# DeltaNet with a max-out network: state times keys and queries in one product of 128 stationary columns, together with a wider fine solve, a new start and the output in the other half

## Chip, cores and metric

One core of one Trainium2 chip. The metric is the device time of one execution in microseconds. Each kernel was run four to six times (once profiled) beside runs of the kernel before on the same chip. The rounds of experiments ran on different chips, so runs of different rounds are compared by their ratio to the kernel before. "PE" is TensorE, "PEld" its weight loads, "DVE" VectorE, "ACT" ScalarE, "POOL" GpSimd, "SP" SyncE.

## The reference

Four sequences of 768 tokens and 8 heads of 48 go through a delta rule; its output, 3072 tokens of 384, goes through a max-out network with three input matrices and one output matrix.

```python
for t in range(S):                       # S = 768, D = 48, per batch (4) and head (8)
    y[:, :, t] = einsum('bhd,bhde->bhe', q_t, state)
    v_old = einsum('bhde,bhd->bhe', state, k_t)          # k normalized
    state = state + beta_t * einsum('bhd,bhe->bhde', k_t, v_t - v_old)
x = y.transpose(0, 2, 1, 3).reshape(B * S, H * D)
out = maximum(maximum(x @ w1, x @ w2), x @ w3) @ w_out
```

## The kernel before

The sequence is cut into 12 chunks of 64 tokens. Two chunks make a group of 512 tokens for the feed-forward network (FFN); six groups follow each other. The FFN products of one group (`p_h`, `p_o`) are mixed with the delta-rule links of the next two chunks. A chunk needs the inverse of a triangular matrix: DVE solves small diagonal blocks, then PE puts the blocks together (`p_e`, `p_f`, the "fine solve", and `p_z`, `p_j`). Then the state is multiplied with the chunk's keys (`p_k`) and queries (`p_q`); the first is subtracted from the values, the second kept for the output.

```python
def times_state(kqt, i, name):            # i = 0: keys, 1: queries
    p_b = ps_two(name)
    for j in range(NP):
        for g in range(2):
            for par in range(2):
                for bb in range(2):
                    c0 = (g * NP + j) * D
                    nc.tensor.matmul(
                        p_b[rows(bb), par, c0 : c0 + D],
                        kqt[g][rows(par), j, bb ^ g, i],   # 64 rows x 64 columns, stationary
                        st[rows(par), bb ^ g, g, j],       # 64 rows x 48 columns, moving
                    )
    return p_b[...]
...
def old_k(c):                             # one subtraction on DVE, 128x768
    ... out=rhs, in0=rhs, in1=times_state(kqt, 0, "p_k"), op=ALU.subtract
def old_q(c):                             # one copy on ACT, 128x768
    ... nc.scalar.copy(heads(qs), times_state(kqt, 1, "p_q"))
...
# start: the fine solves of chunks 0 and 1 are interleaved, ahead of the first FFN product
halves_z(0); halves_u(0); halves_z(1); join_z(0); halves_u(1); join_u(0); join_z(1)
old_k(0); old_q(0); new(0); join_u(1); to_y(0); to_x(0)
```

(The last three lines are shortened: weight conversions and loads between them are left out.) `rows(0)` and `rows(1)` are the two halves of 64 partitions, so the four combinations of `par` and `bb` use four tiles of 64x64 of the PE array.

## Time and profile before

| | before |
|---|---|
| time, median of 4 runs | 616.4 us (615.9 to 617.9) |
| first FFN product `p_h` starts | 76.0 us |
| `p_e` of chunk 2 starts | 127.8 us |
| last `p_o` of the first group ends | 210.7 us |
| from there to the last `p_o` of the sixth group | 399.5 us |
| granted clock after 155.7 us | 1.0 without a break up to 613.1 us |

The times in the table are read from the start and end of single instructions in the trace. The last two rows are a steady part in which PE is busy 98% of the time, at full clock.

### The profile page before, as it was taken

The numbers are of one execution on the slowest core, as the hardware profiler recorded it, in microseconds if no ns is written. First come the engines' busy times: TensorE is split into PE (matmuls) and PEld (weight loads), VectorE is DVE, ScalarE is ACT, GpSimd is POOL, SyncE is SP. The second block draws the span as 40 slices with busy tenths as digits, with TensorE's granted clock in tenths as the row PEclk, the third lists the DMA queues.
The fourth block names the chain that finished last, engine by engine and source line by source line (L and its number), as shares of the span: only waits on it lengthen the run. The fifth ranks groups of instructions, "written<-read, shape, count | busy, mean of one in ns | idle before, by whom it ended". The sixth has DMA issues, their size and how long they took to land.

```text
span 614.8 us, 19609 instructions
## 1 busy us (share of the span) xinstructions
PE 559.4 (91%) x8794; PEld 342.7 (56%) x8794; DVE 304.8 (50%) x713; ACT 160.8 (26%) x292; POOL 77.4 (13%) x108
## 2 busy tenths in 40 slices
PE   6644667978999999999999999999999999999996
PEld 5534556867655665555655546655556455554443
DVE  1652599328739962389542499432595422101110
ACT  3231545236613142121233121232111111110000
POOL 5360274114400000000000000000000000000000
PEclk9655569897999999999999999999999999999999
DMA  8985257652673254421452321522103100010002
GB/s 156 178 203 123 73 137 141 137 145 70 125 123 65 48 121 74 87 49 31 90 105 58 63 54 27 108 54 61 21 14 82 28 2 3 13 39 1 0 1 52
DMA packets 140820, 45.46 MB, mean 74 GB/s; under 512 B 126400, under 2 KB 136384, under 8 KB 140736
## 3 DMA queue, kind: packets, MB, share of 16 engines
q1 hardware_dynamic: 137744, 41.45, 33.2%
q0 software_dynamic: 880, 2.36, 1.4%
q8 instruction: 69, 1.13, 0.8%
q10 hardware_dynamic: 2112, 0.39, 0.4%
q14 instruction: 15, 0.12, 0.1%
HBM read 29.98 MB, written 14.16 MB: 72 GB/s over the span
## 4 chain that ended last, share of the span: by engine, by line
PE 70%; DVE 16%; issue 5%; POOL 3%; DMA 2%; SPq 2%; ACT 1%; POOLq 0%; ACTq 0%; DVEq 0%
PE p_h L707 37%; PE p_o L731 15%; DVE y_bl L453 4%; DVE tmp L449 4%; PE p_g L356 3%; PE p_t L334 3%; PE p_k L597 2%; DVE h L717 1%; PE p_q L597 1%; PE p_y L660 1%; PE p_z L564 1%; SPq L112 1%; PE p_s L643 1%; PE p_u L625 1%; PE p_e L521 1%
## 5 line engine op out<-in xcount | busy, mean ns | idle before, releaser
L707 PE MATMUL p_h<-xt,w_sb 128*128 128x512 f32 (+1 forms) x702 | 301.3, 575 | 2.0 <-DVE xt L693 1.3
L707 PEld LDWEIGHTS p_h<-xt,w_sb 128*128 128x128 f32 x702 | 130.9, 195 | 124.8 <-issue 116.6
L717 DVE TENSOR_TENSOR h<-h,p_h 128x512 f32<-128x512 f32 (+1 forms) x78 | 50.2, 644 | 142.9 <-PE p_h L707 142.8
L731 PE MATMUL p_o<-wo_sb,h 128*128 128x384 f32 x288 | 97.1, 490 | 2.5 <-DVE h L717 2.4
L731 PEld LDWEIGHTS p_o<-wo_sb,h 128*128 128x128 f32 x288 | 53.3, 190 | 41.3 <-DVE h L717 6.5
L453 DVE TENSOR_TENSOR y_bl<-y_bl,tmp 128x31 f32<-128x31 f32 (+20 forms) x154 | 52.7, 342 | 4.2
L449 DVE TENSOR_TENSOR tmp<-x_bl,y_bl 128x31 f32<-128x31 f32 (+20 forms) x154 | 51.8, 337 | 4.2
L715 ACT COPY h<-p_h 128x512 f32<-128x512 f32 (+1 forms) x39 | 21.5, 551 | 122.1 <-PE p_h L707 122.1
L356 PE MATMUL p_g<-kqt 64*64 64x64 f32 (+1 forms) x1280 | 32.1, 249 | 11.0 <-ACT kqt L340 10.5
L275 POOL TENSOR_TENSOR v_t<-v_t,nrm 128x768 f32<-128x768 f32 x12 | 18.2, 1513 | 180.7 <-DMA v_t<-in_v_dram 93.7
L356 PEld LDWEIGHTS p_g<-kqt 64*64 64x64 f32 x1280 | 27.6, 149 | 18.1 <-ACT kqt L340 14.0
L739 ACT COPY o_sb<-p_o 128x384 f32<-128x384 f32 x24 | 11.5, 480 | 88.3 <-PE p_o L731 85.3
L340 ACT COPY kqt<-p_t 128x512 f32<-128x512 f32 (+1 forms) x32 | 25.2, 797 | 31.2 <-PE p_t L334 31.0
L509 DVE STREAM_TRANSPOSE t<-ut 32x256 f32<-32x256 f32 x32 | 13.9, 434 | 23.1 <-DMA ut<-y_d 22.8
L236 POOL TENSOR_TENSOR w_sb<-mant,up 128x384 int32<-128x384 int32 x18 | 18.7, 1036 | 20.6 <-DVE mant L232 11.6
L334 PE MATMUL p_t<-ident,kpad 128*128 128x128 f32 x96 | 17.0, 308 | 4.3 <-DVE pt L366 2.1
L366 DVE TENSOR_TENSOR pt<-p_g,mask 128x512 f32<-128x512 f32 x24 | 16.1, 686 | 9.1 <-PE p_g L356 8.8
L374 ACT COPY at<-p_g 128x512 f32<-128x512 f32 x20 | 11.6, 586 | 32.2 <-DVE pt L366 29.7
L213 POOL TENSOR_SCALAR mant<-mant 128x384 f32<-128x384 f32 x24 | 12.7, 531 | 51.9 <-ACT mant L209 51.8
L625 PEld LDWEIGHTS p_u<-v_t,ut 64*64 64x64 f32 x768 | 13.2, 142 | 8.9 <-issue 7.7
L334 PEld LDWEIGHTS p_t<-ident,kpad 128*128 128x128 f32 x96 | 12.5, 156 | 8.8 <-issue 5.5
L643 PEld LDWEIGHTS p_s<-u,kpad 64*64 64x64 f32 x704 | 12.2, 144 | 9.1 <-issue 5.3
(97 smaller groups left out, 503.1 us busy)
## 6 DMA issues: line engine op xcount, KB each, us to landing
w_bits<-in_moe_w_dram SPq DMA_DIRECT2D x18, 384.0 KB, 3.6
at_d<-at SPq DMA_DIRECT2D x36, 128.0 KB, 2.5
qpad<-in_q_dram SPq DMA_DIRECT2D x48, 96.0 KB, 3.1
v_t<-in_v_dram SPq DMA_DIRECT2D x24, 192.0 KB, 4.3
out_dram<-o_sb SPq DMA_DIRECT2D x48, 96.0 KB, 2.2
kpad<-in_k_dram SPq DMA_DIRECT2D x44, 96.0 KB, 3.4
x_bl<-at_d SPq DMA_DIRECT2D x22, 128.0 KB, 3.6
y_d<-y_bl SPq DMA_DIRECT2D x11, 256.0 KB, 3.0
```

The costliest lines, as they stand in the source:

```text
L236: nc.gpsimd.tensor_tensor(out=dst.bitcast(I32), in0=mant_v.bitcast(I32), in1=up_v, op=ALU.add)
L334: nc.tensor.transpose(p_t[:, i, j * 128 : (j + 1) * 128], src[:, 2 * j : 2 * j + 2], ident,)
L340: nc.scalar.copy(kqt.rearrange("p j b i t -> p i (j b) t")[:, some], p_t.rearrange("p i (x t) -> p i x t", t=C)[:, some],)
L356: nc.tensor.matmul(p_g[rows(bb ^ (g * i)), par, c0 : c0 + C * (1 + whole)], kq[:, 0], kq if whole else kq[:, i],)
L449: nc.vector.tensor_tensor(out=t_v, in0=row.to_broadcast(t_v.shape), in1=column.to_broadcast(t_v.shape), op=ALU.mult,)
L453: nc.vector.tensor_tensor(out=rest, in0=rest, in1=t_v, op=ALU.subtract)
L597: nc.tensor.matmul(p_b[rows(bb), par, c0 : c0 + D], kqt[g][rows(par), j, bb ^ g, i], st[rows(par), bb ^ g, g, j],)
L625: nc.tensor.matmul(p_v[rows(bb ^ g), g, h], ut[c % NU][rows(bb), g, h], rhs[rows(bb), g, h],)
L707: nc.tensor.matmul(p_h, w_sb[i][:, t, f * 128 : (f + 1) * 128], xt[:, t, lo : lo + w], start=(t == 0), stop=(t == KT - 1),)
L715: nc.scalar.copy(h, p_h)
L717: nc.vector.tensor_tensor(out=h, in0=h, in1=p_h, op=ALU.max)
L731: nc.tensor.matmul(p_o, hs[f][:, i * 128 : (i + 1) * 128], wo_sb[:, f], start=(f == 0), stop=(f == FT - 1),)
```

## The change

Its intent is to halve the number of products of state with keys and queries, by taking keys and queries side by side as one stationary operand of 128 columns. Queries then come out in the other half of the partitions, so the output moves there too. With it come four other edits: the fine solve works on tiles of 64 rows in place of 32; chunk 1's solve moves behind the first FFN product; PE's order in the first group is fixed by hand; most weight fetches are issued by ACT, and the loads of beta by POOL. Smaller ones are not shown: the fine solve writes its tile without four copies on ACT, the turned keys and queries are copied in two pieces, loads of the start are in another order, and 18 products of no use, which keep PE busy at the start, stand in place of 24.

```diff
-    def times_state(kqt, i, name):
-        ... (64 columns, once for keys, once for queries; one eviction each)
+    def old(c):
+        ...
+        for g in range(2):
+            p_b = ps_two("p_b")
+            ...
+            for j in range(NP):
+                for par in range(2):
+                    for bb in range(2):
+                        kq = kqt[g][rows(par), j, bb ^ g]
+                        nc.tensor.matmul(
+                            p_v[:, par, bb, j],
+                            kq.rearrange("p i t -> p (i t)"),   # 128 columns
+                            st[rows(par), bb ^ g, g, j],
+                        )
+            for bb in range(2):        # evictions: 64 partitions x 384 each
+                ... nc.scalar.copy(to[r_q], p_v[r_q, :, bb])
+            for bb in range(2):
+                ... nc.vector.tensor_tensor(out=rhs, in0=rhs, in1=p_v[r, :, bb], op=ALU.subtract)
 (fine solve)
-                        r = block(bb, f)                          # 32x32, 16 columns
-                        nc.tensor.matmul(p_v[r, g, h], at[g][r, h, BL*f : BL*(f+1)], d[r, g, h, HB:])
+                r = rows(bb)                                      # 64x64, 32 columns
+                nc.tensor.matmul(p_v[r, g, h], at[g][r, h], second[r, g, h, :, 1])
 (output)
-                    p_v[rows(bb), g, h], pt[g][rows(bb ^ g), h], ...
+                    p_v[rows(1 - bb), g, h], pt[g][rows(bb ^ g), h], ...
 (start)
-    halves_z(1) ... halves_u(1) ... join_z(1) ... join_u(1)       # before the first FFN product
+    FIRST = {0: "s0 e1 T2", 1: "f1 P2 T3", 2: "z1 P3", 3: "k1 j1", ...}   # behind it
+    by_hand.enter_context(tc.manual_schedule(engines={mybir.EngineType.PE}))  # first group
-            nc.sync.dma_start(out=st...)      # fetch of weights
+            queue.dma_start(out=st...)        # queue = nc.scalar
```

## The prediction

> **What bounds the kernel now.** I read the stage table (busy time of each engine in chosen stretches) first, cut where the chain of waits shows the phases change: the triangular solve of chunks 0 and 1 (40 to 75.4 us), the first feed-forward group up to chunk 2's state product (to 119.6), the rest of that group (to 206.8), and groups 1 to 5.
>
> ```profile
> core 0: us, PE busy (x) PEld busy (x) DVE busy (x) ACT busy (x) POOL busy (x), PEclk, DMA share, GB/s
> 40.00:75.40 35.40, 19.20 (x934) 17.06 (x934) 12.15 (x24) 12.77 (x25) 9.14 (x14) 0.50 0.49 108
> 75.40:119.60 44.20, 34.55 (x672) 27.79 (x674) 35.86 (x83) 18.60 (x39) 20.72 (x24) 0.82 0.66 136
> 119.60:206.80 87.20, 81.06 (x1783) 55.21 (x1784) 54.52 (x130) 34.30 (x68) 19.31 (x22) 0.92 0.50 106
> 206.80:614.80 408.00, 400.25 (x5032) 221.67 (x5031) 182.19 (x419) 81.64 (x135) 11.84 (x9) 1.00 0.23 47
> ```
>
> After 206.8 us PE is busy 98% at full clock: any PE time added or removed there moves the end one for one. Before that PE has holes and a low clock, and DVE (36 of 44 us) is the limit between 75 and 107 us, where the chain runs along it. So the change has to be judged twice: in a latency-bound start and in a PE-bound rest.
>
> The chain of waits in the start shows how the first solve spends its time:
>
> ```profile
> 46.11 1.03 PE p_f L541 x59
> 47.14 1.65 issue
> 48.78 1.09 PE p_f L541 x67
> ...
> 50.68 2.25 issue
> 52.94 0.99 PE p_e L521 x46
> ...
> 54.78 3.80 issue
> ```
>
> The "issue" pieces, with 1.57 and 2.12 us more up to 66 us, make 11.4 us in which PE waits for nothing that the profile shows, among streams of very small products.
>
> For the product in question I read the timeline and then the groups by form:
>
> ```profile
> 474.32 1.15 PE L597 MATMUL p_k<-st,kqt 64*64 64x48 f32 x64
> 475.29 1.11 PE L597 MATMUL p_q<-st,kqt 64*64 64x48 f32 x64
> 476.33 1.98 PE L707 MATMUL p_h<-xt,w_sb 128*128 128x512 f32 x4
> ```
>
> ```profile
> L707 PEld LDWEIGHTS p_h<-xt,w_sb 128*128 128x128 f32 x702 | 130.9, 195 | 124.8 <-issue 116.6 <-DVE h L717 0.9 <-DVE x_bl L435 0.5
> L597 PEld LDWEIGHTS p_k<-st,kqt 64*64 64x64 f32 x704 | 11.3, 135 | 7.2 <-issue 6.1 <-DVE h L717 0.8 <-DVE t L527 0.3
> L564 PEld LDWEIGHTS p_z<-ut,at 32*32 32x32 f32 x512 | 5.3, 105 | 3.0 <-issue 3.0
> ```
>
> A product of the program is two MATMULs here (64 for the 32 in p_k). Keys and queries together take 476.33 - 474.32 = 2.01 us a chunk, 15.7 ns an instruction. p_h streams 512 columns in 0.43 us (2.58 us for six in the chain), 0.84 ns a column, so 48 columns would be 40 ns, or 10 ns an instruction with four tiles at work. The moving side is therefore not the limit. A weight load lasts 105, 135 and 195 ns for 32, 64 and 128 columns: about 0.9 ns for each stationary column, on top of a fixed part. 64 columns are some 55 to 60 ns, and a quarter of that is the 15 ns seen. **The product is bound by loading stationary columns, four tiles side by side.**
>
> [...]
>
> **The change part by part.**
>
> 1. State times keys and queries: 32 products a chunk with 128 stationary columns instead of 64 with 64. Half the instructions, but each loads 128 columns[...]. [...] **+1.6 us a chunk**, 11 chunks. Eight fall to groups 1 onward: **+12.8 us**, all on the path. Three fall to the start.
>
> 2. Its evictions: one subtraction (950 ns) and one copy (799 ns) of 128x768 become four each of 64 partitions x 384, about 0.55 and 0.48 us (a 128x384 copy takes 480 ns). That adds 1.25 us on DVE and 1.1 on ACT a chunk. Chunks with five microseconds of FFN work before their next product hide it, but DVE is nearly full in each group that still solves (7.5 of 8 us between 266 and 274), where PE already waits 1.0 us for it: about 1 us for each of three groups, **+3 us**. The split kqt copies (two of some 0.6 us for one of 1.0) are hidden.
>
> 3. Fine solve: 64 products a stage on 32-row blocks become 32 with 64 columns in two diagonal tiles. Instructions halve (512 to 256 MATMULs for two chunks' p_e), fill's four ACT copies (0.615 us each) go. PE time per stage rises: 64 x 29 ns = 1.9 us at full clock against about 1.1 now, twice that cold. DVE gains a second 0.71 us transpose.
>
> 4. Start: y_d and its read-back all go through SP. Now POOL issues half of them behind v_t, mant and w_sb work (dg at 39.9 us, first p_e at 43.0 to 43.7). I expect ut0 at 41 to 42. Chunk 1's solve leaves the path to the first FFN product. Chunk 0 alone, largely cold: p_e 3.5, copy 0.6, p_f 3.5, corners 1, p_z 1, transposes and copy 2.5, p_j and its eviction 2, p_u 1.7, u 0.6, p_y 1.7, y 0.6, p_x and xt 2, waits for DVE's in-order queue 1.5 and issue holes 1.5: 24 us, first p_h near 65 instead of 75.4, **10 us earlier**.
>
> 5. What takes this back: chunk 1's solve and its DVE work now fall into the DVE-bound stretch. Counting DVE's program order with the present mean times, from first p_h to the end of solve 1: 12 weight conversions 12.9, solve 8.7, transposes and corners 4.0, masks 2.8, h 2.5, norms and sums 4.8, state, y and v updates 4.1, joins and memsets 3.2, gaps 3: 46 us against 30 now (the same count gives what the trace shows, 75 to 105). Solve 1 ends near 111 instead of 105. Its result needs some 7 us of DMA, so p_e of chunk 2 starts near 118; now it starts at 127.8, since PE had other work. So the 10 us survive this point. After it PE has 3.6 us more in p_e and p_f and 1.6 in the state product, but the 13 us of holes there (3.4 of issue, the rest behind conversions on POOL and DVE) should fall by about 5, as conversions finish earlier. Net there: 0.
>
> Sum: 616 - 10 + 12.8 + 3 = **622 us**.
>
> **Rivals.** (A) The cost follows instructions, not columns: 64 instructions at 15.7 ns take 1.0 us, and the term of +12.8 becomes -8. Then about 598 to 602. For it: "issue" holes among small products. Against it: 32-column products run 128 MATMULs in 1.3 us, 10 ns each, faster than 64-column ones, so instructions are not the floor. I give it 12%. (B) The start gains much more, because manual PE order removes most of the 28 us that PE is idle (16) or slowed by its clock (12, from the stage table) between 75 and 207 us: 605 to 612. Against it stands DVE's count; 25%. (C) The start gains nothing: ACT, in order, now waits for staging buffers when it issues fetches, delays the kqt copies, and cold PE doubles the longer p_e and p_f: 630 to 638. For it: ACT issue of some 0.6 us each, 20 fetches; 20%. (D) Two row tiles do not overlap, since two products on the same tile follow each other: 5 us or more a chunk, above 640. p_g of odd units has the same order and still runs at 15 ns; 5%.
>
> **Range and chances.** The column argument is well supported and the start is the uncertain half, about 10 us either way. 8 in 10: 606 to 636. Two per cent are 603.6 and 628.2. Faster needs (A), or (B) at its best; slower is a start that gains under 4 us, or (D). Faster 0.09, within 0.60, slower 0.31.
>
> **What would show each step.** p_b: 64 MATMULs in 3.4 to 3.8 us in steady state (1.0 to 1.3 would make A right). Length of a middle group: 87.5 us now, near 91.5 after. First p_h near 65 us. Solve 1 ending near 111, p_e of chunk 2 near 118, first group's end near 197. DVE above 80% busy from first p_h to 110 us. I am wrong if the middle groups do not get longer, or if the first group ends more than 10 us from 197.

## The result, and the profile after

The changed kernel took **637.8 us** (median of 4, 635.0 to 641.4) against 616.4 us: ratio 1.0346, 95% interval 1.029 to 1.040. It is slower, and lies 1.8 us outside the range that was given. In the later table every ratio is to the kernel before, run beside it.

The stage table of the changed kernel, cut at its first `p_h`, at `p_e` of chunk 2 and at the end of the first group. (The prediction's table has its second cut earlier, at chunk 2's state product; its last row is cut at the same event.) From here on a product is one MATMUL of the trace, two of which make a product of the program.

```profile
core 0: us, PE busy (x) PEld busy (x) DVE busy (x) ACT busy (x) POOL busy (x), PEclk, DMA share, GB/s
40.00:67.70 27.70, 18.82 (x426) 16.24 (x424) 11.45 (x24) 9.15 (x20) 8.61 (x13) 0.50 0.60 130
67.70:126.80 59.10, 49.45 (x888) 41.52 (x890) 47.28 (x109) 34.03 (x78) 27.97 (x37) 0.88 0.91 183
126.80:210.80 84.00, 80.05 (x1371) 53.99 (x1372) 60.81 (x148) 22.19 (x49) 9.90 (x8) 0.94 0.31 56
210.80:639.60 428.80, 423.32 (x4520) 238.73 (x4518) 188.70 (x426) 90.70 (x170) 7.53 (x5) 0.98 0.22 45
```

The last row is 428.8 us against 408.0 before. Two things are in it. PE's busy time rose by 23 us although it runs fewer products (4520 against 5032). And the granted clock is 0.98, where it had been 1.00.

The timeline of PE at one chunk of the changed kernel (start and length in us, engine, line, operation, tile, shapes, count):

```profile
447.56 3.81 PE L599 MATMUL p_b<-st,kqt 64*128 64x48 f32 x64
451.30 7.09 PE L708 MATMUL p_h<-xt,w_sb 128*128 128x512 f32 x12
```

The 64 products take 451.30 - 447.56 = 3.74 us, where `p_k` and `p_q` together took 2.01. Behind them, twelve `p_h` take 7.09 us. Twelve take 5.42 elsewhere. The row of the granted clock (in tenths, 40 slices) shows it over the whole run, first before, then after:

```profile
PEclk9655569897999999999999999999999999999999
```

```profile
PEclk9655797888989999999899899999899898999999
```

Each 8 behind the first group is a stretch of exactly 3.41 us in which the clock was 0.5. In the trace there are five of them after 210 us, from 311.35, 359.14, 451.30, 495.67 and 536.63 us on, and every one begins within 0.7 us of a state product's end. PE was not idle ahead of them. The stage table around two state products of the changed kernel, one followed by a drop and one not:

```profile
355.00:359.20 4.20, 4.20 (x63) 3.45 (x62) 1.09 (x2) 0.94 (x2) 0.00 (x0) 0.99 0.42 65
359.20:362.60 3.40, 3.40 (x11) 1.76 (x10) 1.80 (x4) 0.94 (x2) 0.00 (x0) 0.51 0.00 0
...
400.90:404.60 3.70, 3.70 (x65) 3.65 (x64) 2.46 (x5) 1.53 (x3) 0.00 (x0) 1.00 0.77 146
404.60:408.00 3.40, 3.40 (x16) 1.86 (x14) 2.85 (x6) 0.94 (x2) 0.00 (x0) 1.00 0.57 101
```

PE is busy in the whole of each stretch (4.20 of 4.20 us and 3.70 of 3.70 us in the first lines), and yet the granted clock behind the first product is 0.51 and behind the second 1.00.

The start, in the same order of events:

| | before | after | predicted |
|---|---|---|---|
| first `p_h` | 76.0 | 67.7 | 65 |
| DVE part of the second solve ends | 106.2 | 113.5 | 111 (where it has 105 before) |
| `p_e` of chunk 2 | 127.8 | 126.7 | 118 |
| first group ends (last `p_o` ends) | 210.7 | 214.6 | 201 (197 in the prediction, where it is 206.8 before) |
| from there to the last `p_o` | 399.5 | 420.4 | |

So the first FFN product does come 8 us earlier, and little of it (1 us) is left at chunk 2's `p_e`. The end of the second solve is read from SP, which sends its result to `y_d` as soon as DVE is done, and fetches it back in the layout that PE needs. Before, then after:

```profile
106.30 1.13 SPq L458 DMA_DIRECT2D y_d<-y_bl  x2
110.30 5.15 SPq L469 DMA_DIRECT2D dg<-y_d  x8
```

```profile
113.57 1.13 SPq L461 DMA_DIRECT2D y_d<-y_bl  x2
117.42 3.49 SPq L470 DMA_DIRECT2D ut<-y_d  x4
```

### The profile page after: what moved, and what is told of

Read it like the earlier page. It is cut to its first block, busy times and chain, and to the rows that moved or that the text cites. A ratio compares the mean times of both kernels' runs of the same rounds, so it can differ in the third digit from the quotient of the medians.

```text
span 639.6 us, 17274 instructions
## 1 busy us (share of the span) xinstructions
PE 595.5 (93%) x7566; PEld 370.8 (58%) x7566; DVE 327.3 (51%) x763; ACT 168.9 (26%) x349; POOL 71.6 (11%) x102
## 4 chain that ended last, share of the span: by engine, by line
PE 77%; DVE 13%; DMA 4%; issue 2%; ACT 2%; SPq 1%; POOL 1%; ACTq 0%; DVEq 0%; POOLq 0%
PE p_h L708 42%; PE p_o L732 14%; PE p_b L599 5%; DVE y_bl L457 3%; DVE tmp L453 3%; PE p_g L360 3%; PE p_t L337 3%; PE p_u L621 2%; PE p_y L659 2%; DMA qpad<-in_q_dram 2%; PE p_e L520 2%; PE p_s L642 1%; PE p_f L538 1%; PE p_j L571 1%; DVE h L718 1%
## 5 line engine op out<-in xcount | busy, mean ns | idle before, releaser
L708 PE MATMUL p_h<-xt,w_sb 128*128 128x512 f32 (+1 forms) x702 | 312.4, 593 | 1.2 <-DVE xt L694 1.2
L708 PEld LDWEIGHTS p_h<-xt,w_sb 128*128 128x128 f32 x702 | 134.8, 201 | 128.1 <-issue 118.4
L716 ACT COPY h<-p_h 128x512 f32<-128x512 f32 (+1 forms) x39 | 21.6, 553 | 127.5 <-PE p_h L708 126.7
L599 PEld LDWEIGHTS p_b<-st,kqt 64*128 64x128 f32 x704 | 40.8, 188 | 7.5 <-issue 6.7
L599 PE MATMUL p_b<-st,kqt 64*128 64x48 f32 x704 | 42.3, 275 | 0.0
L347 ACT COPY kqt<-p_t 128x256 f32<-128x256 f32 (+1 forms) x64 | 27.0, 482 | 26.3 <-PE p_t L337 26.3
L611 DVE TENSOR_TENSOR v_t<-v_t,p_b 64x384 f32<-64x384 f32 x44 | 24.3, 552 | 15.8 <-ACT qs L607 15.0
L740 ACT COPY o_sb<-p_o 128x384 f32<-128x384 f32 x24 | 11.4, 477 | 78.7 <-PE p_o L732 76.1
L607 ACT COPY qs<-p_b 64x384 f32<-64x384 f32 x44 | 20.8, 473 | 41.5 <-PE p_b L599 40.7
L504 DVE STREAM_TRANSPOSE t<-ut 32x256 f32<-32x256 f32 x48 | 20.8, 433 | 6.3 <-DMA ut<-y_d 5.5
L337 PE MATMUL p_t<-ident,qpad 128*128 128x128 f32 x96 | 16.6, 300 | 5.2 <-DMA qpad<-in_q_dram 4.5
L621 PE MATMUL p_u<-v_t,ut 64*64 64x48 f32 x768 | 16.4, 234 | 4.8 <-DVE v_t L611 2.9
```

Source lines behind the costliest of these rows:

```text
L337: nc.tensor.transpose(p_t[:, i, j * 128 : (j + 1) * 128], src[:, 2 * j : 2 * j + 2], ident,)
L347: nc.scalar.copy(to[:, :, some], of[:, b])
L599: nc.tensor.matmul(p_v[:, par, bb, j], kq.rearrange("p i t -> p (i t)"), st[rows(par), bb ^ g, g, j],)
L611: nc.vector.tensor_tensor(out=rhs, in0=rhs, in1=p_v[r, :, bb], op=ALU.subtract)
L621: nc.tensor.matmul(p_v[rows(bb ^ g), g, h], ut[c % NU][rows(bb), g, h], rhs[rows(bb), g, h],)
L708: nc.tensor.matmul(p_h, w_sb[i][:, t, f * 128 : (f + 1) * 128], xt[:, t, lo : lo + w], start=(t == 0), stop=(t == KT - 1),)
```

## The experiments

Eighteen further runs were made, one of them the changed kernel again. The names in the headings are used below. Two theories were held first. **Columns and clock**: the wide product costs 1.73 us a chunk because it loads 128 columns on two tiles, and its length brings the clock down. **Start**: something takes the start's 8 us back. All results in one table:

| run | time, us (median) | ratio to before | 95% interval |
|---|---|---|---|
| changed kernel, first / again | 637.8 / 637.7 | 1.0346 / 1.0311 | 1.029-1.040 / 1.025-1.037 |
| e1_split | 634.8 | 1.0285 | 1.024-1.033 |
| e2_four_tiles | 618.6 | 1.0017 | 0.998-1.005 |
| e3_only_state | 646.7 | 1.0463 | 1.044-1.048 |
| e4_moving_96 | 637.0 | 1.0331 | 1.027-1.039 |
| s1_sync | 617.1 | 0.9988 | 0.995-1.003 |
| s2_halves | 625.2 | 1.0125 | 1.009-1.016 |
| s3_later | 616.5 | 0.9986 | 0.994-1.003 |
| s4_halves_later | 621.4 | 1.0060 | 1.003-1.009 |
| t1_ahead | 624.5 | 1.0129 | 1.008-1.018 |
| t2_warm | 618.8 | 1.0021 | 0.996-1.008 |
| u1_free | 619.1 | 1.0019 | 0.999-1.005 |
| u2_free_warm | 617.3 | 0.9993 | 0.996-1.003 |
| u3_free_ahead | 619.1 | 1.0018 | 0.999-1.005 |
| u4_sync_later_warm | 619.2 | 1.0005 | 0.996-1.005 |
| v1_light (wrong) | 620.3 | 1.0038 | 1.000-1.008 |
| v2_before_light (wrong) | 616.7 | 0.9984 | 0.996-1.001 |
| w1_beta | 618.2 | 1.0013 | 0.999-1.004 |

### The product on four tiles again: e2_four_tiles

```diff
-    nc.tensor.matmul(p_v[:, par, bb, j], kq.rearrange("p i t -> p (i t)"), st[...])
+    for i in range(2):
+        nc.tensor.matmul(p_v[rows(i), par, bb, j], kq[:, i], st[...])
```

> The changed kernel, with each product of 128 stationary columns written as two products of 64 columns into the same places of PSUM (64 products become 128 a chunk; layout, evictions, schedule and start as in the changed kernel). Column theory: the product of a chunk falls from 3.74 to about 2.0 us, 11 chunks behind the end of the first group and three before it are worth 8 x 1.73 = 14 us in the steady part and the five clock drops there (8.5 us) go too: 638 - 14 - 8.5 - some 2 in the first group = about 613 us. Rival A of the prediction (cost follows the number of instructions): it becomes slower than the changed kernel, 645 to 655 us. Rival C (the start is what was lost, the product costs little): within 3 us of 638.

It took 618.6 us. Of PE at one chunk:

```profile
473.90 2.12 PE L600 MATMUL p_b<-st,kqt 64*64 64x48 f32 x128
475.95 7.99 PE L709 MATMUL p_h<-xt,w_sb 128*128 128x512 f32 x18
```

Twice as many instructions take 475.95 - 473.90 = 2.05 us, and 18 `p_h` behind them 7.99 us, which is full clock. There is no drop in the whole steady part. That part is 400.6 us, 1.1 us longer than before. **The whole loss of the changed kernel, some 3%, is the wide product and what follows from it.** What remains, the rest of the change, is worth nothing: 1.0017. I had expected 613 us, as I still credited part of the start.

### The product alone, on the kernel before: e3_only_state

The edit puts `old` of the diff above, the turned copies and the output half into the kernel before, and the first output product ahead of the second state product, which this edit needs.

> The kernel before with the state product alone changed (one product of 128 stationary columns for keys and queries, keys and queries turned in two copies, output in the other half, the first output product ahead of the second state product, as it needs); start, schedule of the first group and halves of the inverse as before. Column theory with clock theory: 616 + 11 to 14 chunks x 1.73 us (19 to 24, of which 14 in the steady part) + clock drops 5 to 6 x 1.7 us (8 to 10): 640 to 648 us, so the rest of the change wins some 5 us. Without clock drops: 632 to 636. Rival A: 600 to 612 us.

It took 646.7 us, as the column and clock theories said. Its steady part is 420.6 us, the same as in the changed kernel (420.4), with five drops again. Its first group ends at 219.9 us, against 214.6 in the changed kernel, so with the wide product the rest of the change does win something (1.0463 against 1.0346 and 1.0311), most of it in the first group. I did not follow that further.

### Which side bounds it: e4_moving_96

```diff
-    st[rows(par), bb ^ g, g, j],
+    st[rows(par), bb ^ g, g, j : j + n],      # n = 2 for j < 3: 96 columns
```

> The changed kernel, with the moving side of the state product widened from 48 to 96 columns for three of each four products (two heads' states at once; the columns that are too many are written over by the next product, so the result stays right). Tells which side bounds the 64 tiles of 3.74 us. If loading the 128 stationary columns bounds [...]: the product stays at 3.7 to 4.0 us, the time at 635 to 640 us, and perhaps fewer clock drops, as more rows are multiplied. If the streaming of the moving side bounds, with two row tiles not overlapping: 16 x 48 + 48 x 96 columns against 64 x 48, so 1.75 times 3.74 = 6.5 us, and 660 us or more.

The view of the tile `p_b` in this run (count, then shortest, median and longest in ns, first and last start, shapes), and one chunk on its timeline:

```profile
L600 PE MATMUL p_b<-st,kqt x704: 232/272/527, 91.4 to 532.4; 64*128 64x96 f32 x132, 64*128 64x48 f32 x44
```

```profile
446.45 3.85 PE L600 MATMUL p_b<-st,kqt 64*128 64x96 f32 x64
450.23 5.42 PE L709 MATMUL p_h<-xt,w_sb 128*128 128x512 f32 x12
```

With 1.75 times the moving columns it takes 450.23 - 446.45 = 3.78 us, against 3.74. The moving side costs next to nothing here. Half as many instructions took nearly twice as long (3.74 us for 64 against 2.05 for 128 in e2_four_tiles), so it is not their number either: of these three costs, what is left is the loading of weights. Its records are longer too, 188 ns for a load of 64x128 in the changed kernel against 134 ns for one of 64x64 in e2_four_tiles. There were no drops in the steady part (414.1 us), and at first I took that for the effect of more rows multiplied. The next experiment says why that does not follow.

### The clock: e1_split and the changed kernel again

```diff
-    10: "y0", 11: "k1", ...
+    10: "y0 K1", 11: "L1", ...     # K: products of g = 0, L: of g = 1, one FFN step between
```

> The changed kernel, with the state product of a chunk issued as its two halves (32 tiles each), one step of the feed-forward network between them, in groups 1 to 7 of the links. Nothing is added or taken away. Column theory with clock theory (the 64 tiles of a chunk take 3.74 us because a tile of 128 stationary columns loads in twice the time; and so long a stretch of few multiply rows drops the granted clock to 0.5 for 3.41 us behind it, about 1.7 us each, five or six times): the two halves still take 3.7 us together, and the drops behind them are gone, so some 8.5 us less than the changed kernel, near 629 us. Rival (the drops have another cause, the low clock is due to the sum of the work): the drops stay, the time stays at 636 to 639 us.

> The changed kernel unchanged, as a control beside the others: ratio to the kernel before 1.030 to 1.040 as first measured, and again five drops of the granted clock to 0.5 behind state products in the steady part, give or take one. If the drops were chance, their number differs by more than two.

In e1_split the two halves of a chunk:

```profile
447.78 2.02 PE L602 MATMUL p_b<-st,kqt 64*128 64x48 f32 x32
449.74 2.84 PE L711 MATMUL p_h<-xt,w_sb 128*128 128x512 f32 x6
452.51 2.02 PE L602 MATMUL p_b<-st,kqt 64*128 64x48 f32 x32
454.46 5.42 PE L711 MATMUL p_h<-xt,w_sb 128*128 128x512 f32 x12
```

The products take as long as before (1.96 and 1.95 us), all `p_h` run at full clock, and no drop is left in the steady part: 414.2 us against 420.4 in the changed kernel. So five drops cost 6.2 us net. The time falls by 0.3 to 0.6% (1.0285 against 1.0311 and 1.0346), which the intervals do not separate; some 629 us had been expected, and 634.8 came. The profile says why so little is left: the first group ends at 219.5 us in e1_split and at 214.6 in the changed kernel, so most of what the steady part wins is lost ahead of it. That loss was not followed.

The control run of the changed kernel had three drops in the steady part where the first had five (steady part 418.6 us), so their number varies. The trace tells why. All changes of the granted clock within one profile lie at multiples of 3.413 us from each other. From the first of the five drops in the changed kernel to the second it is 14 of them, then 27, 13 and 12. So within a profile the clock changes at the edges of a window of 3.413 us with a fixed phase. I compared the start of each of the 33 unsplit state products of the changed kernel, its control and e3_only_state with these window edges. In all 16 cases with a drop an edge lay between 0.14 us before and 0.60 us after the start of the product, so that one window fell almost wholly into it. In all 17 cases without a drop the next edge came 0.82 to 3.15 us after the start. **In these runs a state product of 3.7 us (64x128 tiles, 48 moving columns) that fills one window, or nearly, was followed by one window at half clock, in 16 cases of 16; products of 2 us, shorter than a window (halves in e1_split, 64x64 tiles in e2_four_tiles), had no drop behind them in the steady part.** In e4_moving_96 the next edge came 0.67 us or more after the start in every case, so its lack of drops may be chance. Whether more moving columns would keep the clock up stays open.

### Where the start's gain went: six edits of the four-tile version

All of these build on e2_four_tiles, so that only the start differs from the kernel before.

**s1_sync**: `fetch(queue=nc.sync)` in place of `nc.scalar`. **s3_later**: no conversion and fetch in steps 1, 3, 5 and 7 of the first group, two each in steps 12 to 15.

> The four-tile version (618.6 us, in its profile first p_h at 68.2, p_e of chunk 2 at 127.0, first group end at 209.0), with every weight fetch issued by SP instead of ACT. Why did the start gain nothing, though first p_h comes 8 us earlier than in the kernel before? Rival C of the prediction (ACT is held when it issues fetches): p_e of chunk 2 near 121, time near 612 us. Theory (what was gained is chunk 1's solve moved behind first p_h, some 7 us of PE work, and ACT waits in order for w_bits to land, 9.8 us in all, whoever issues them): p_e of chunk 2 within 2 us of 127, time within 3 us of 618.6.

> The four-tile version, with the weight conversion and its fetch left out in steps 1, 3, 5 and 7 of the first feed-forward group and made up by two each in steps 12 to 15. Each conversion is 1.03 us of DVE and 1.1 us of ACT in the stretch in which DVE is over 90% busy and ACT waits for w_bits (76 to 110 us). Theory (the conversions crowd DVE and, by ACT's order, hold the evictions of chunk 1's solve): PE's idle time of 12 us between 80 and 127 us falls by 3 to 5, p_e of chunk 2 at 122 to 124, time 613 to 616 us. Rival (the chain of solve 1 alone sets it, or the weights come too late now): no gain, or p_h waiting for w_sb, 618 to 622 us.

Both moved the time by less than their intervals. Rival C of the prediction (ACT is held by issuing fetches) is out. The conversions alone are not it either.

**s2_halves**: the fine solve on 32-row blocks again, 128 products of 16 moving columns in place of 64 of 32. **s4_halves_later** adds the later conversions.

```diff
-    r = rows(bb);          at[g][r, h],           second[r, g, h, :, 1]
+    r = block(bb, f);      at[g][r, h, w],        u_t[r, g, h, w][:, HB:]     # w: 32 columns
```

> The four-tile version, with the two products of the fine solve (p_e, p_f) on blocks of 32 rows and 16 moving columns, as in the kernel before, in place of blocks of 64 rows and 32 columns; same layout, evictions and schedule. 64 columns cost 3.6 us a product at half clock and 2.0 warm against 1.9 and 1.1. Theory (PE's work until the end of the first group is what a chunk of that stage costs, since PE is 94% busy from 127 us on): first p_h 3.4 us earlier (near 65), products of chunks 2 and 3 together 3.6 us shorter, first group end 4 to 6 us earlier, time near 614 us. Rival (other engines set the first group's end): first p_h earlier, end within 1.5 us of the four-tile version.

> Both at once: fine solve on blocks of 32 rows, and four conversions made later, on the four-tile version. If both theories hold and their gains add: 618.6 - 4.5 - 4 = 610 us, faster than the kernel before by 1.2%. If the two take away the same wait: as the better of the two alone.

I expected a gain of 4 us from s2_halves and got a loss of 6.6. Both theories fell. With the short products the later conversions do win something (1.0125 to 1.0060), which they did not with the wide ones. The timeline of s2_halves behind its first `p_h` (in brackets the idle time just before, and its end):

```profile
68.71 1.93 PE L648 MATMUL p_s<-u,kpad 64*64 64x48 f32 x64
70.56 1.18 PE L521 MATMUL p_e<-ut,at 32*32 32x16 f32 x119
76.27 0.34 PE L521 MATMUL p_e<-ut,at 32*32 32x16 f32 x9 [4.53 <-issue]
```

The short products are done sooner, but PE then stands for 4.53 us in which it waits for nothing that the profile's waits show ("issue"), as in the start of the kernel before.

The packets of the DMA queue `q8 instruction` in the kept traces point to what it waits for. The line below is of the kernel before: 69 packets of 16 KB for the 17588 MATMULs and weight loads of PE, which makes 255 to a packet.

```profile
q8 instruction: 69, 1.13, 0.8%
```

In s2_halves one such block landed at 74.88 us and PE went on at 76.27. In the kernel before, PE stands for 1.65, 2.25, 3.80, 1.57 and 2.12 us in its first solve (the 11.4 us of "issue" in the prediction) and for 1.03 and 2.33 us behind 132 us. Each of these seven holes ends 1.3 to 1.6 us after a block has landed, and from one to the next within a solve PE runs 255 or 256 instructions. So it looks as if PE runs out of instructions in streams of very short ones. The four-tile version, with half as many in the fine solve, has no such hole of over 1 us inside it. No run tested this further.

From the first `p_h` to 149 us the granted clock of s2_halves was 0.5 in 42 of 83 us, against 14 of 81 in the four-tile version. So the wide fine solve is a true gain in this order, 6.6 us.

**t1_ahead**: chunk 1's solve ahead of the first `p_h`, interleaved with chunk 0's as in the kernel before. **t2_warm**: 20 more 128x128 products of no use in PE's waits ahead of the first solve.

> The four-tile version, with the solve of chunk 1 (p_e, p_f, p_z, p_j) put ahead of the first feed-forward product again, interleaved with chunk 0's, as the kernel before has it. In the four-tile version it stands behind first p_h, which comes 8 us earlier for that (68.2 against 76.0), and yet p_e of chunk 2 is at 127.0 in both. Theory (PE's fixed order makes it the same work in another place; earlier first p_h is no gain): first p_h 5 to 9 us later (73 to 77), p_e of chunk 2 within 3 us of 127, time 614 to 621 us. Rival, the prediction's step (10 us earlier first p_h reaches the end): time 5 us or more longer than the four-tile version, 624 us or more.

> The four-tile version, with 20 more 128x128 products of no use on PE in its waits of 33 to 44 us, so that the array is busy when the first solve begins; the granted clock was 0.5 from 23.7 to 71.5 us. If the clock follows the activity just before: some of p_e(0), p_f(0) run at full clock (2.0 in place of 3.6 us), first p_h 2 to 4 us earlier. Theory (first p_h does not set the end): time within 2 us of 618.6. Rival (it does): 614 to 616 us.

t1_ahead cost some 7 us by its ratio (1.0129 against 1.0017). That was named as the rival's case, so in this fixed order the earlier first `p_h` is worth something. t2_warm says the opposite: `p_e` and `p_f` of chunk 0 took 2.50 and 2.77 us instead of about 3.6 each, the first `p_h` came at 64.4 us, 3.8 us earlier, and the median did not move (618.8). Single runs went from 614.6 to 622.6, so 2 us either way stay open. In its profile the first group ends 3.9 us earlier than in the four-tile version, and of that 1.9 us are left at the last `p_o`.

### Order free, and engines relieved

**u1_free** drops the fixed PE order of the first group; **u2_free_warm** and **u3_free_ahead** do the same to t2_warm and t1_ahead; **u4_sync_later_warm** adds up three harmless edits.

```diff
-    by_hand = ExitStack()
-    by_hand.enter_context(tc.manual_schedule(engines={mybir.EngineType.PE}))
     for i, _ in enumerate(ffn(0)):
```

> The four-tile version (618.6 us), without the fixed order of TensorE in the first feed-forward group, so that the scheduler places its products, as in the kernel before; all else as it is. Theory M (the fixed order makes PE wait for products whose operands come late, 12 us between 80 and 127 us, and is what takes the start's gains back): PE's waits there fall by half, time 610 to 614 us. Rival (DVE and ACT set that stretch, whatever PE's order): within 2 us of 618.6. Rival (the fixed order helps, as it keeps chunk 2 early): 621 us or more.

> As u1_free, with chunk 1's solve ahead of the first feed-forward product as in t1_ahead: the kernel nearest to the one before that has the wide fine solve. If theory M holds and the wide fine solve is a gain in that order too: 610 to 614 us. If it stays at 620 to 625 us as t1_ahead, the fixed order is not the cost, and the wide fine solve is no gain where two chunks are interleaved.

> As u1_free, with the 20 idle products ahead of the first solve as in t2_warm. t2_warm's profile had its first group end 3.9 us earlier than the four-tile version, its median none. If that was chance: as u1_free. If the warm start counts where PE is not held in order: 2 to 4 us less than u1_free.

> The four-tile version with three small changes that did no harm each: fetches issued by SP (ratio 0.9988), four conversions later (0.9986), and the idle products ahead of the first solve (1.0021, best profile). If their gains add: 613 to 615 us. If each was noise: 616 to 618 us.

All four are within 0.2% of the kernel before. With the order free, chunk 1's solve ahead or behind makes no difference (619.1 both), so t1's 7 us belonged to the fixed order. The small gains did not add.

**v1_light** and **v2_before_light** leave out one of DVE's two instructions of each weight conversion, in the four-tile version and in the kernel before. Their outputs are wrong, which doesn't matter for the times.

> The four-tile version, with one of the two DVE instructions of each weight conversion left out (the mask and shift, 24 of about 0.43 us, 10 us in all, of which some 6 between 68 and 110 us). The result is wrong on purpose. Theory D (DVE, nearly full from first p_h to the end of solve 1, pins the start): first group end 5 us or more earlier, time 611 to 614 us. Rival (PE's own work and waits on data set it): within 2 us of 618.6.

> The kernel before, with the same instruction left out; wrong on purpose. Theory D holds for both kernels, with as large a gain or less here: 611 to 615 us. If the kernel before gains nothing and the four-tile version does, DVE became the limit only with the change, and the start's gain was lost there.

DVE's row of the stage table for v1_light, from first products to the end of the second solve:

```profile
68.00:110.00 42.00, 34.87 (x758) 28.71 (x758) 33.20 (x77) 22.47 (x53) 19.44 (x25) 0.74 0.84 170
```

DVE went from 38.66 us in this stretch (four-tile version) to 33.20, and neither kernel gained. That was my favourite by then, and the prediction's own reading ("DVE is the limit between 75 and 107 us"). So these 5.5 us of DVE are worth nothing at the end. DVE as a limit is not excluded by that: from 85 to 114 us, where the second solve runs, it was still busy for 25.5 of 29 us in v1_light (28.0 in the four-tile version), and the solve ended 43.2 us after the first `p_h` instead of 45.1.

**w1_beta**: s1 and s3 together, and the loads of beta issued by SP first, as before.

> The four-tile version with the load of beta issued by SP as the first transfer of the start, as in the kernel before (in the changed kernel POOL issues it, ahead of the gather of x_bl), and with the two edits that seemed to help a little, fetches issued by SP and four conversions later. In the profiles of 13 versions with the changed start the first solve's first product (tmp) is at 27.0 to 29.9 us, in those with the start of before at 25.7 to 26.5. Theory F (this late begin is the last part of what took the start's gain back): tmp at 25.5 to 26.5, first group end 2 to 3 us earlier than in s1_sync and s3_later (208.1 and 210.5), time 612 to 615 us, faster than the kernel before by 0.4 to 0.9%. Rival (what is won early is lost in later waits, as with all other edits of the start): 616 to 619 us.

No gain, and its mechanism failed too: the first solve still began at 29.2 us (25.8 before).

## Why the prediction was wrong, point by point

**1. State product: right.** +1.6 us a chunk was predicted from columns loaded, and 3.4 to 3.8 us for 64 products. Measured: 3.74 us, +1.73, so 13.8 us for eight chunks against 12.8. The weight load of 128 columns is what e2_four_tiles and e4_moving_96 leave as the bound (half the instructions took 3.74 in place of 2.05 us, 1.75 times the moving columns 0.04 us more). The 1.6 us were the author's estimate: the trace before has no stream of 64x128 tiles. An estimate from its numbers alone, with two tiles loading side by side, comes close as well: four tiles at 15.7 ns an instruction are 62.8 ns a load of 64 columns, and a load of 128 columns lasts 60 ns longer (195 against 135 ns), which makes 123 ns for a pair and 3.9 us for 64 products. Measured were 3.74 / 32 = 117 ns a pair. Rivals A (cost follows instructions) and D (no overlap, 5 us or more) are out.

**2. Evictions: about 1 us where +3 were put down, but not sharply measured.** The steady parts without a clock drop of e1_split (414.2) and e4_moving_96 (414.1) are 14.6 to 14.7 us longer than before, which leaves 0.8 to 0.9 us beside the 13.8. The four-tile version has the same evictions and its steady part is 1.1 us longer. But the same later code took from 400.3 to 402.7 us in the ten four-tile profiles without a drop there, so a cost of up to 3 us is not excluded.

**3. Missing: the clock.** The prediction did not ask what a *busy* stretch of 3.7 us with 48 moving columns does. (Its stage table has 0.50 in the first solve, where PE was busy for 19.2 of 35.4 us.) Five drops cost 6.2 us in the steady part of the profiled run (e1_split). With points 1 and 2 that makes 13.8 + 1.1 + 6.2 = 21.1 us; 20.9 were measured (420.4 - 399.5); so close a fit is partly luck, given the spread in point 2.

**4. The start: the step that failed.** "So the 10 us survive this point" is wrong. The profiled run of the changed kernel is 24.8 us longer than that of the kernel before, 19 us more than the sum (+5.8): 14 of them are here (first group +4.0 in place of -10), 5 in the steady part. Even with the product on four tiles, the term of -10 measured about -1: the same start ends its first group 1.0 us before the kernel before, and the time is the same within 0.5%. The prediction's own sign of being wrong, a first group that ends more than 10 us from 197, came true.

What failed in its terms are two waits. The end of DVE's second solve was nearly right (113.5, +7.3 us against the kernel before, where 111 and +6 were predicted). But "Its result needs some 7 us of DMA" was too short: SP sent the result at 113.57 us, chunk 2's pieces of `ut` were issued from 117.42 to 121 us, and three whose landing the trace shows came in at 121.6, 123.0 and 123.2. In the four-tile version the last came in at 125.2. So `p_e` of chunk 2 could not start at 118 in any order of PE. In the kernel before the last of the eight pieces for two chunks landed at 118.1 and PE was late for other work, as the prediction says. Secondly, "the 13 us of holes" after this point, of which 5 were to go, were not there: PE is idle for 6.1 us from 127.8 to 206.8 us of the kernel before.

Of the rest of the start, the sum of 24 us for chunk 0 was right (43.4 to 67.7 us), but its first `p_e` came at 43.4 us and not soon after 41 to 42. (The 512 MATMULs of `p_e` in the prediction are those of four chunks, not two.)

The first `p_h` was a bad marker. It came 8 us sooner because chunk 1's solve was put behind it. The stage table of the kernel before and of the four-tile version, from first `p_h` to `p_e` of chunk 2 and on to 210 us:

```profile
76.00:127.00 51.00, 41.95 (x824) 34.47 (x825) 36.73 (x85) 19.97 (x42) 20.57 (x24) 0.85 0.67 141
127.00:210.00 83.00, 76.86 (x1637) 50.40 (x1636) 56.01 (x134) 33.25 (x67) 19.31 (x22) 0.92 0.46 98
```

```profile
68.00:127.00 59.00, 46.51 (x1016) 38.63 (x1016) 50.37 (x113) 34.18 (x78) 28.61 (x37) 0.88 0.88 183
127.00:210.00 83.00, 78.39 (x1449) 52.12 (x1449) 61.48 (x160) 22.89 (x51) 9.47 (x7) 1.00 0.33 59
```

The 8 us that the first stretch is longer hold 4.6 us more PE work and 3.4 us more PE idle time (12.5 against 9.1). Nor is 127 us the same point of the work in both. From there on the four-tile version still has 36 `p_h` of 256 columns to do against 28, and 256 `p_g` against 192. It makes that up because none of it runs at half clock, while the kernel before has 13.7 us at 0.5 in this stretch (mean 1.00 against 0.92).

What makes the data late and holds PE up in this stretch is not settled. In the four-tile version the largest single waits behind the first `p_h` are 3.2 us on DVE (`p_z`), 2.9 us on ACT's `kqt` copies and 2.3 us on ACT ahead of `p_u`, but taking away one suspected cause at a time (fetch queue, early conversions, fixed order, part of DVE's work, cold clock, loads of beta) brought no change beyond 0.4%, and several at once none either. Not tried is less data: DMA is 88% busy from 68 to 127 us against 67% from 76 to 127 before, the eight pieces of the second solve take 4.3 us from issue to landing against 3.0 before (medians), and ACT waits 9.8 us between 40 and 128 us for weights to land. That is the remaining suspect, not a finding.

**5. Chances.** "Slower" had 0.31, put down to a start that gains under 4 us. That did happen. But a start worth zero alone gives 616 + 12.8 + 3 = 632 us; the last 6 us were the clock, which no rival had. The sum of rival C (630 to 638) holds the result, but by luck: its mechanism was refuted by s1_sync.

No version was faster than the kernel before beyond its interval. The best, s3_later and s1_sync, are equal to it (0.9986 and 0.9988).

## What to carry to other kernels

Merging two products into one with 128 stationary columns halves the instructions and may still cost nearly twice the time (here 3.74 against 2.01 us): with few moving columns, count the columns loaded per tile and the tiles that work side by side. A stream like this one (64x128 tiles, 48 moving columns, 3.74 us) was followed by 3.41 us at half clock in 16 of 33 cases; split into pieces of 2 us by other products it had no drop behind it in the steady part. Other shapes were not tried, but for the one of e4_moving_96. Where PE stops among very short products and no wait is shown, look at when its blocks of instructions land (here seven such holes ended 1.3 to 1.6 us after a landing). And a milestone that comes earlier is a gain only if the work put behind it was not needed for the next one; mark progress by a point that both versions reach with the same work done.
